# An attention recurrence fused with a Gelu MLP: decays computed in place, another order for the ramp, and two transposes moved to the DMA queue

## The chip, the cores and the metric

The kernel runs on one core of one Trainium2 chip. The metric is the device time of one execution, in microseconds, and a time quoted below is a median of several executions. TensorE is called PE, its weight loads PEld, VectorE DVE, ScalarE ACT, GpSimd POOL, and SyncE (which issues every DMA here) SP. Runs have a fast and a slow state (slower by over 1.5%, or at a lower granted clock). All ratios below are of fast runs; a median may hold a slow run, and then the text says so.

## The reference

A decaying key-value state is updated for every time step, read by `r`, and the result goes through a two-layer MLP. Shapes: 4 batches, 8 heads, 768 steps, head dimension 48; the MLP is 384 to 2048 to 384.

```python
for t in range(S):
    cur = einsum('bhd,bhe->bhde', u * k[t], v[t])
    y[t] = einsum('bhd,bhde->bhe', r[t], state + cur)
    state = w[t][..., None] * state + einsum('bhd,bhe->bhde', k[t], v[t])
x = y.transpose(0, 2, 1, 3).reshape(B * S, H * D)      # 3072 x 384
h = x @ w_in
g = 0.5 * h * (1.0 + tanh(c * (h + 0.044715 * h**3)))  # Gelu
out = g @ w_out
```

## The kernel before

The work is cut into 12 units, each of 256 time steps of one batch. Each of the 128 partitions holds an even and an odd step (`t2` = 0 and 1). A unit has an attention half and an MLP half. The MLP half of unit q (`mm1`, Gelu, `mm2`) is interleaved on PE with the attention half of unit q+1 (steps a2 to a6), and the decays of a later unit are prepared beside both.

The decays become exponentials of cumulative sums of log w. `x` sums up to before the even step, `y` through the even step, `z` through the odd step. `k` is scaled by exp(-y) or exp(-z), `r` by exp(x) or exp(y):

```python
    def a1(q):
        lw = logws[q % 3]
        x, y, z = (ps_a.tile([P, 512], FP, tag="a", name=f"cum{q}_{i}") for i in range(3))
        for dst, s0, s1 in ((x, strict, strict), (y, incl, strict), (z, incl, incl)):
            PE.matmul(dst[:, 0:HD], s0, lw[:, 0, :, 0:D], start=True, stop=False)
            PE.matmul(dst[:, 0:HD], s1, lw[:, 1, :, 0:D], start=False, stop=True)
        for g in range(G):
            for t2 in range(2):
                PE.matmul(z[:, ds(HD + 2 * g, 2)], lw[:, t2, ds(2 * g, 2), :], ones2,
                          start=False, stop=(t2 == 1), skip_group_check=True)
        st["cum", q] = (x, y, z)

    def exps(q):            # cut: the tiles fq, e1 and al are in SBUF
        ...
        ACT.activation(out=e1[:, 0, :], in_=y[:, 0:HD], func=AF.Exp, scale=-1.0)
        ACT.activation(out=e1[:, 1, :], in_=z[:, 0:HD], func=AF.Exp, scale=-1.0)
        ACT.activation(out=fq[:, 0, :], in_=x[:, 0:HD], func=AF.Exp)
        ACT.activation(out=fq[:, 1, :], in_=y[:, 0:HD], func=AF.Exp)
        ACT.activation(out=al, in_=z[:, ds(HD, 2 * G)].rearrange("p (g c) -> p g c", c=2),
                       func=AF.Exp)
            # cut

    def prep(q):            # cut
        ...
        DVE.tensor_tensor(out=kk[:, :, :, 0:D], in0=tdh(kt), in1=dec(e1), op=AL.mult)
        DVE.tensor_tensor(out=rq[:, :, :, 0:D], in0=tdh(rt), in1=dec(fq), op=AL.mult)
        # cut: POOL makes vb (a cast of v), rk = r*k*u, and am, the state's decay
        ...

    def prep_b(q):
        kk, rq, vb, vsc, am = st["pre", q]
        rk, dg = st.pop(("diag", q))
        DVE.tensor_reduce(out=dg, in_=rk, axis=AX.X, op=AL.add)
        POOL.tensor_tensor(
            out=vsc, in0=vb,
            in1=dg.rearrange("p h t -> p t h")[:, :, :, None].broadcast_to([P, 2, H, D]),
            op=AL.mult)
```

`kk` and `rq` are transposed on PE through PSUM, and DVE copies the result back:

```python
    def a2(q, which):
        kk, rq, vb, vsc, am = st["pre", q]
        src = (kk, rq)[which]
        ps = ps_a.tile([P, G, 2, 2, 64], BF, tag="a", name=f"T{q}_{which}")
        for g in range(G):
            for t2 in range(2):
                PE.transpose(ps[:, g, :, t2, :], src[:, t2, ds(2 * g, 2), :], ident)
        dst = pw2.tile([P, G, 2, 2, 64], BF, tag=f"T{which}", name=f"TT{q}_{which}")
        DVE.tensor_copy(out=dst, in_=ps)
        st["T", q, which] = dst

```

The first units are the ramp. There the weights still arrive and are cast to bf16, and the order of the program is different (casts of `w_out` follow the whole of `mm1`; the Ln and the sums of unit 2 come last):

```python
    for q in range(NU):
        if q + 3 < NU:
            for nm in ("k", "r", "v"):
                load(q + 3, nm)
        if q + 4 < NU:
            load(q + 4, "w")
        att = attention(q + 1) if q + 1 < NU else iter(())
        table("gelu")
        ramp = q < 2
        if ramp:
            for i in range(8):
                mm1(q, i)
            if q == 0:
                for i in range(8):
                    cast_w_out(i, DVE if i in (0, 3, 6) else (ACT if i in (1, 4, 7) else POOL))
        for i in range(8):
            if not ramp:
                mm1(q, i)
            if i >= 2:
                mm2(q, 0, (2 * i - 4, 2 * i - 3))
            if i in (1, 3, 4, 5, 6, 7):
                next(att, None)
            if i == 6 and 0 < q and q + 2 < NU:
                a1(q + 2)
        table("exp")
        if q == 0:
            ln(2)
            a1(2)
        if q + 2 < NU:
            exps(q + 2)
        # cut: rest of mm2, stores, prep(q + 2), prep_b(q + 2)
```

## Time and profile before

| | before |
|---|---|
| time, median of 3 runs (lowest to highest) | 236.93 us (235.68 to 237.95) |
| span of the profiled run, mean granted clock | 235.9 us, 0.968 |
| PE busy | 203.4 us, 86% |
| distance from one unit's first mm1 matmul to the next, units 4 to 7 | 16.56 us |
| first mm1 matmul of units 0, 1, 2, 3 | 24.78, 53.74, 74.04, 91.34 us |

The page's slice view cuts the span into 40 equal slices. A digit is the busy share in tenths (9 is 90% or more), and PEclk is the granted clock in tenths. Before:

```profile
PE   0456787598895999999999999999999999999992
...
PEclk9999996779997999999999999999999999999998
```

From slice 13 on (the first is slice 0; this is at 77 us) PE is at 9. In slices 6 and 7 (35 to 47 us) and in slice 12 it falls to between 5 and 7, and there the clock is at 6 or 7 tenths. So there are two regimes: a steady one in which PE's own work sets the time, and a ramp in which PE waits and is also slow. The chain of waits, by engine, says the same: PE is only about half of what ended last.

```profile
PE 54%; ACT 19%; DVE 11%; issue 9%; POOL 3%; DMA 2%; DVEq 0%; ACTq 0%; POOLq 0%
ACT L156 5%; DVE w_out_sb L86 2%; DMA w_89<-in_w_dram 2%; PE o_0_532 L354 1%; DVE rq_127 L203 1%; ACT logw_124 L162 1%; PE o_0_3678 L354 1%; PE o_0_3457 L354 1%; PE o_0_3175 L354 1%; PE o_1_3740 L354 1%; PE o_1_3632 L354 1%; PE o_1_3389 L35
```

The first line is the share of the span by engine, the second by line and tile. The second gives 5% to the loading of the Exp table (L156), 2% to DVE casts of `w_out`, and 1% to a Ln (`logw_124`). The table load comes in every unit; the casts are entries of the ramp alone.

The windows view gives one steady unit of before and the 15 us in which the clock is low. Columns: the window and its length, then busy us with the number of instructions in brackets for PE, PEld, DVE, ACT and POOL, then the granted clock, the DMA share and GB/s.

```profile
35.00:40.00 5.00, 3.24 (x56) 1.51 (x56) 4.21 (x7) 0.55 (x1) 1.12 (x2) 0.67 1.10 248
40.00:45.00 5.00, 3.42 (x40) 2.13 (x41) 2.96 (x3) 1.99 (x3) 4.40 (x3) 0.65 1.12 255
...
124.47:141.03 16.56, 15.89 (x210) 11.42 (x208) 10.18 (x17) 10.51 (x20) 8.22 (x6) 1.00 0.54 121
```

A steady unit holds 15.89 us of PE work in 16.56 us. Between 35 and 50 us the clock is two thirds and PE is busy for only 10.5 of 15 us (the third slice, left out, has 3.82 us and 0.69). The Trainium skill, "TensorE: Matmul & The Clock Gate", Part 1: The HAM clock gate, says that the throttled clock is the default and that activity releases it. This trace agrees. From 26.4 us to the end of PE's work, the granted clock is 0.50 in three stretches, which start at 36.67, 46.90 and 74.21 us and last 6.8, 3.4 and 3.4 us. Each starts within 0.8 us of the end of one of PE's three longest waits of that time (2.1 us to 36.68, 2.7 us to 46.18 and 2.4 us to 74.04). Ahead of 26.4 us the column has no record and reads full speed, but PE is slow there too: the matmuls of the first sums start 0.32 us apart (at 5.71 and 6.03 us), and those of unit 2, of the same shape, 0.16 us apart (at 46.18 and 46.34 us).

The two longest of PE's waits between 25 and 74 us (columns: engine, tile and line, who released it; us in total, times, longest) name what the ramp waits for:

```profile
PE cum_0_658 L170 <- ACT logw_124 L162: 2.7, 1, 2.7
PE mt_0_0_537 L249 <- DVE TT_0_530 L238: 2.1, 1, 2.1
```

The first is unit 2's sums waiting for its Ln. The second is the scores of unit 1 waiting for the copy of its transposed tile. On DVE's timeline (start, us, engine, line, operation) that copy stands behind three casts of `w_out`:

```profile
32.50 1.84 DVE L86 CAST w_out_sb<-wo_179 128x768 bf16<-128x768 f32 x1
34.26 1.17 DVE L86 CAST w_out_sb<-wo_187 128x768 bf16<-128x768 f32 x1
35.36 0.68 DVE L238 COPY TT_1_519<-T_1_510 128x1024 bf16<-128x1024 bf16 x1
35.96 0.67 DVE L238 COPY TT_0_530<-T_0_521 128x1024 bf16<-128x1024 bf16 x1
```

These are the second and third cast (the first, 1.09 us, starts at 31.49), and the two copies. The second copy is the one that PE waits for.

In the steady state the trace has two small holes per unit on PE, here in the unit from 124.47 us (the bracket is idle time and what ended it):

```profile
127.19 0.81 PE L345 MATMUL h_2_1987<-xT_1899,w_in_sb 128*128 128x256 bf16 x6 [0.36 <-ACT g_1948 L347]
...
135.36 0.32 PE L170 MATMUL cum_1_2151<-logw_123,incl 128*128 128x384 bf16 x1 [0.31 <-ACT xs_2148 L321]
```

The first, 0.36 us, is mm1's third group waiting for the Gelu to free a PSUM buffer. The second, 0.31 us, is the second of the three sums waiting for a PSUM buffer that ACT reads. The Gelu is late because ACT is in its other table. ACT's timeline of that block:

```profile
121.50 1.28 ACT L156 ACT_TABLE_LOAD   x1
122.80 0.49 ACT L183 ACTIVATE e_1880<-cum_1_1847 128x384 bf16<-128x384 f32 x1
...
125.25 1.28 ACT L158 ACT_TABLE_LOAD   x1
```

From the first table load (121.50) to the end of the second (126.53) ACT is away from the Gelu for 5.0 us.

### The profile page before, as it was taken

The page shows a single profiled execution, that of the slowest core. Times are in us where ns is not written, and L with a number is a line of the kernel's source. Part 1 is how long each engine was busy: PE and PEld are TensorE (multiplying, and loading weights), DVE is VectorE, ACT ScalarE, POOL GpSimd, SP SyncE. Part 2 cuts the span into 40 slices and gives each one's busy share as a digit, 9 for nine tenths or more (in the row PEclk, how much of TensorE's full clock was granted, in tenths as well). Part 3 has the DMA queues.
Part 4 walks back from the last instruction along what each step waited for, and adds up shares of the span by engine and source line. Part 5 has one row for each costly group of instructions (what it writes and reads, how often), then busy time and mean ns, then how long its engine had stood idle before and what let it go on. Part 6 is the DMA issues. An engine that isn't in the chain of part 4 may idle for free.

```text
span 235.9 us, 5759 instructions
## 1 busy us (share of the span) xinstructions
PE 203.4 (86%) x2448; PEld 143.0 (61%) x2448; DVE 131.3 (56%) x211; ACT 134.0 (57%) x223; POOL 104.5 (44%) x87
## 2 busy tenths in 40 slices
PE   0456787598895999999999999999999999999992
PEld 0334564357564767667767667676777677677761
DVE  7684686561636538547547747656285376374200
ACT  3433780566255449459368377395494684765670
POOL 3473792639008504806708509329158076060000
PEclk9999996779997999999999999999999999999998
DMA  7999999713902911942923914915719120020202
GB/s 173 307 396 297 331 320 255 160 33 72 231 15 54 246 25 36 206 98 53 232 56 75 257 24 111 210 33 124 182 35 212 24 62 10 13 56 0 68 1 67
DMA packets 56969, 30.45 MB, mean 129 GB/s; under 512 B 50928, under 2 KB 56176, under 8 KB 56944
## 3 DMA queue, kind: packets, MB, share of 16 engines
q1 hardware_dynamic: 56944, 30.09, 52.1%
q8 instruction: 19, 0.31, 0.6%
q14 instruction: 6, 0.05, 0.1%
HBM read 25.36 MB, written 4.72 MB: 127 GB/s over the span
## 4 chain that ended last, share of the span: by engine, by line
PE 54%; ACT 19%; DVE 11%; issue 9%; POOL 3%; DMA 2%; DVEq 0%; ACTq 0%; POOLq 0%
ACT L156 5%; DVE w_out_sb L86 2%; DMA w_89<-in_w_dram 2%; PE o_0_532 L354 1%; DVE rq_127 L203 1%; ACT logw_124 L162 1%; PE o_0_3678 L354 1%; PE o_0_3457 L354 1%; PE o_0_3175 L354 1%; PE o_1_3740 L354 1%; PE o_1_3632 L354 1%; PE o_1_3389 L354 1%; POOL rk_418 L210 1%; POOL rk_418 L212 1%; ACT logw_122 L162 1%
## 5 line engine op out<-in xcount | busy, mean ns | idle before, releaser
L345 PEld LDWEIGHTS <-w_in_sb 128*128 128x128 bf16 x576 | 54.0, 99 | 21.1 <-issue 9.9
L156 ACT ACT_TABLE_LOAD x13 | 16.7, 1283 | 0.9 <-PEq L487 0.7
L158 ACT ACT_TABLE_LOAD x12 | 15.4, 1283 | 0.2
L171 PEld LDWEIGHTS <-strict 128*128 128x128 bf16 x24 | 2.5, 104 | 9.9 <-issue 9.5
L215 POOL TENSOR_TENSOR am_997<-blk,al_975 128x384 f32<-128x384 bf16 x2 | 2.4, 1230 | 12.5 <-ACT al_975 L187 12.5
L215 POOL TENSOR_TENSOR am_1304<-blk,al_1273 128x384 f32<-128x384 bf16 x2 | 2.4, 1229 | 11.5 <-ACT al_1273 L187 11.5
L215 POOL TENSOR_TENSOR am_1608<-blk,al_1577 128x384 f32<-128x384 bf16 x2 | 2.4, 1230 | 8.3 <-ACT al_1577 L187 8.3
L215 POOL TENSOR_TENSOR am_1912<-blk,al_1881 128x384 f32<-128x384 bf16 x2 | 2.4, 1230 | 8.3 <-ACT al_1881 L187 8.3
L215 POOL TENSOR_TENSOR am_2216<-blk,al_2185 128x384 f32<-128x384 bf16 x2 | 2.4, 1230 | 8.3 <-ACT al_2185 L187 8.3
L215 POOL TENSOR_TENSOR am_2520<-blk,al_2489 128x384 f32<-128x384 bf16 x2 | 2.4, 1228 | 8.3 <-ACT al_2489 L187 8.3
L215 POOL TENSOR_TENSOR am_2811<-blk,al_2780 128x384 f32<-128x384 bf16 x2 | 2.4, 1228 | 7.9 <-ACT al_2780 L187 7.9
L215 POOL TENSOR_TENSOR am_3100<-blk,al_3069 128x384 f32<-128x384 bf16 x2 | 2.4, 1228 | 7.9 <-ACT al_3069 L187 7.9
L215 POOL TENSOR_TENSOR am_3382<-blk,al_3352 128x384 f32<-128x384 bf16 x2 | 2.4, 1228 | 7.9 <-ACT al_3352 L187 7.9
L354 PE MATMUL o_0_532<-w_out_sb,g_437 128*128 128x384 bf16 x16 | 5.5, 469 | 0.2 <-ACT w_out_sb L84 0.2
L236 PEld LDWEIGHTS <-rq_127 128*128 128x128 bf16 x48 | 3.4, 104 | 3.3 <-DVE rq_127 L203 3.2
L354 PEld LDWEIGHTS <-g_437 128*128 128x128 bf16 x32 | 3.3, 117 | 3.2 <-issue 2.5
L170 PE MATMUL cum_0_201<-logw_122,strict 128*128 128x384 bf16 x1 | 0.5, 479 | 5.4 <-ACT logw_122 L162 5.4
L362 DVE COPY ob_3736<-o_0_3678 128x384 f32<-128x384 f32 x1 | 0.6, 558 | 7.7 <-PE o_0_3678 L354 7.7
L215 POOL TENSOR_TENSOR am_699<-blk,al_677 128x384 f32<-128x384 bf16 x2 | 2.3, 1187 | 4.3 <-ACT al_677 L187 4.3
L354 PEld LDWEIGHTS <-g_3653 128*128 128x128 bf16 x32 | 3.0, 98 | 1.7 <-ACT g_3653 L347 0.4
L238 DVE COPY TT_1_818<-T_1_809 128x1024 bf16<-128x1024 bf16 x1 | 0.7, 692 | 6.0 <-PE T_1_809 L236 6.0
L354 PE MATMUL o_0_3678<-w_out_sb,g_3653 128*128 128x384 bf16 x16 | 3.8, 327 | 0.0
(942 smaller groups left out, 694.2 us busy)
## 6 DMA issues: line engine op xcount, KB each, us to landing
wi_155<-in_moe_w_in_dram SPq DMA_DIRECT2D x1, 512.0 KB, 5.0
wi_157<-in_moe_w_in_dram SPq DMA_DIRECT2D x1, 512.0 KB, 6.0
wi_159<-in_moe_w_in_dram SPq DMA_DIRECT2D x1, 512.0 KB, 6.7
wi_161<-in_moe_w_in_dram SPq DMA_DIRECT2D x1, 512.0 KB, 7.5
wi_163<-in_moe_w_in_dram SPq DMA_DIRECT2D x1, 512.0 KB, 8.7
wi_165<-in_moe_w_in_dram SPq DMA_DIRECT2D x1, 512.0 KB, 9.6
w_89<-in_w_dram SPq DMA_DIRECT2D x1, 384.0 KB, 3.7
k_91<-in_k_dram SPq DMA_DIRECT2D x1, 384.0 KB, 4.7
```

The lines of the kernel that those rows point to most:

```text
L86: eng.tensor_copy(out=out, in_=in_)
L156: ACT.preload_act_table_set(EXP_SET)
L158: ACT.preload_act_table(AF.Gelu_apprx_tanh)
L162: ACT.activation(out=lw[:, :, :, 0:D].rearrange("p t h d -> p h t d"), in_=ld.pop(("w", q)).rearrange("p h (t d) -> p h t d", t=2), func=A ...
L171: PE.matmul(dst[:, 0:HD], s1, lw[:, 1, :, 0:D], start=False, stop=True)
L203: DVE.tensor_tensor(out=rq[:, :, :, 0:D], in0=tdh(rt), in1=dec(fq), op=AL.mult)
L210: POOL.tensor_tensor(out=rk, in0=kt.rearrange("p h (t d) -> p h t d", t=2), in1=rt.rearrange("p h (t d) -> p h t d", t=2), op=AL.mult)
L212: POOL.tensor_tensor(out=rk, in0=rk, in1=u_bc[:, :, None, :].broadcast_to([P, H, 2, D]), op=AL.mult)
L215: POOL.tensor_tensor(out=am[:, c2], in0=blk.rearrange("p g j d -> p g (j d)"), in1=al[:, :, c2][:, :, None].broadcast_to([P, G, 2 * D]), o ...
L236: PE.transpose(ps[:, g, :, t2, :], src[:, t2, ds(2 * g, 2), :], ident)
L345: PE.matmul(h[:, f, :], w_in_sb[:, cb, ts(ft, P)], xT[:, cb, :], start=(f + cb == 0), stop=(cb == NCB - 1), skip_group_check=True)
L354: PE.matmul(st["o", q, c2], g[:, ft, ts(c2, P)], w_out_sb[:, ft, :], start=(ft == 0), stop=(ft == NFT - 1))
```

## The change

It has four parts.

1. Two sums and two large Exps instead of three and four. Because y = z - log w(odd) and y = x + log w(even), exp(-y) is exp(-z) times w(odd), and exp(y) is exp(x) times w(even). So `y` is not needed; instead `kw` = k(even) * w(odd) and `rw` = r(odd) * w(even) are computed, on POOL from unit 5 on. With it, mm2 of the unit is moved back by two mm1 groups, so that more PE work follows the table switch.
2. The Exps of all units but unit 5 write in place in PSUM, and DVE's multiplies read them there: four of 384 elements per partition instead of two of 768.
3. The ramp has an order of its own: the decays come earlier, the casts of `w_out` lie between the phases of the attention, loads are issued earlier, and mm1 is interleaved. In the loop behind the ramp, decays run three units ahead instead of two.
4. From unit 6 on (`PE_T`) `kk` and `rq` are transposed by the DMA, issued from SP, instead of by PE and a DVE copy.

The core of the diff; layouts, indices, loads, the start and much of the ramp loop are cut.

```diff
-        x, y, z = (ps_a.tile([P, 512], FP, tag="a", name=f"cum{q}_{i}") for i in range(3))
-        for dst, s0, s1 in ((x, strict, strict), (y, incl, strict), (z, incl, incl)):
-            PE.matmul(dst[:, 0:HD], s0, lw[:, 0, :, 0:D], start=True, stop=False)
-            PE.matmul(dst[:, 0:HD], s1, lw[:, 1, :, 0:D], start=False, stop=True)
+        x, z = ((pool or ps_a).tile([P, 512], FP, tag=tag, name=f"cum{q}_{i}") for i in range(2))
+        for dst, tri in ((x, strict), (z, incl)):
+            for t2 in range(2):
+                PE.matmul(dst[:, 0:HD], tri, lw[:, t2, :, 0:D], start=(t2 == 0),
+                          stop=(t2 == 1))
-        st["cum", q] = (x, y, z)
-
-    def exps(q):
-        x, y, z = st.pop(("cum", q))
-        fq = pw2.tile([P, 2, HD], BF, tag="fq", name=f"fq{q}")
-        e1 = pw2.tile([P, 2, HD], BF, tag="e1", name=f"e1{q}")
-        al = pw2.tile([P, G, 2], FP, tag="al", name=f"al{q}")
-        ACT.activation(out=e1[:, 0, :], in_=y[:, 0:HD], func=AF.Exp, scale=-1.0)
-        ACT.activation(out=e1[:, 1, :], in_=z[:, 0:HD], func=AF.Exp, scale=-1.0)
-        ACT.activation(out=fq[:, 0, :], in_=x[:, 0:HD], func=AF.Exp)
-        ACT.activation(out=fq[:, 1, :], in_=y[:, 0:HD], func=AF.Exp)
-        ACT.activation(out=al, in_=z[:, ds(HD, 2 * G)].rearrange("p (g c) -> p g c", c=2),
-                       func=AF.Exp)
-        st["dec", q] = (fq, e1, al)
         # cut
+    def prep_w(q, eng=POOL):
+        wt, kt, rt = (ld[nm, q] for nm in ("w", "k", "r"))
+        # cut
+        eng.tensor_tensor(out=kw, in0=kt[:, :, 0:D], in1=wt[:, :, D:2 * D], op=AL.mult)
+        eng.tensor_tensor(out=rw, in0=rt[:, :, D:2 * D], in1=wt[:, :, 0:D], op=AL.mult)
         # cut
+    def exps(q, sbuf=False):
+        x, z = (t[:, 0:HD] for t in st["cum", q])
+        zf = st.pop(("cum", q))[1]
+        fq, e1 = x, z
+        if sbuf:
+            fq, e1 = (pw2.tile([P, HD], BF, tag=t, name=f"{t}{q}", bufs=1) for t in ("fq", "e1"))
+        al = pw2.tile([P, G, 2], FP, tag="al", name=f"al{q}", bufs=3)
+        ACT.activation(out=e1, in_=z, func=AF.Exp, scale=-1.0)
+        ACT.activation(out=fq, in_=x, func=AF.Exp)
         # cut
-        DVE.tensor_tensor(out=kk[:, :, :, 0:D], in0=tdh(kt), in1=dec(e1), op=AL.mult)
-        DVE.tensor_tensor(out=rq[:, :, :, 0:D], in0=tdh(rt), in1=dec(fq), op=AL.mult)
+        for dst, t2, x, dec in ((kk, 0, kw, e1), (kk, 1, kt[:, :, D:2 * D], e1),
+                                (rq, 0, rt[:, :, 0:D], fq), (rq, 1, rw, fq)):
+            DVE.tensor_tensor(out=dst[:, :, t2, :, 0:D], in0=gjd(x),
+                              in1=dec.rearrange("p (g j d) -> p g j d", g=G, j=2),
+                              op=AL.mult)
         # cut: a2
+        if q < PE_T[which]:
+            # cut: the transposes on PE and the copy, as before
+            return
+        for c2 in range(2):
+            SP.dma_start(out=dst[:, c2].rearrange("p g t x -> p (g t) x"),
+                         in_=src[ds(64 * c2, 64)].rearrange("p g t j d -> p (g t j d)"),
+                         transpose=True)
         # cut
+    for q in range(3):
+        att = attention(q + 1)
+        table("gelu")
+        for i in range(6):
+            mm1(q, i)
+        if q == 0:
+            wo(0, DVE)
+        next(att)
+        mm1(q, 6)
+        mm1(q, 7)
+        table("exp")
+        prep_b(q + 1)
+        if q > 0:
+            prep_a(2 * q + 1)
+        if q == 2:
+            prep_w(5)
+        if q == 0:
+            wo(1, DVE)
+        if q == 0:
+            ln(2)
+        next(att)
+        if q == 0:
+            wo(2, DVE)
+            wo(3, POOL)
+        mm2(q, 0, (0, 1))
+        next(att)
+        mm2(q, 0, range(2, 6))
+        if q == 0:
+            wo(4, DVE)
+            wo(5, POOL)
+        next(att)
+        mm2(q, 0, range(6, 10))
+        next(att)
+        mm2(q, 0, range(10, 12))
         # cut: rest of the ramp loop
+    for q in range(3, NU):
         att = attention(q + 1) if q + 1 < NU else iter(())
         table("gelu")
         # cut
         for i in range(8):
+            mm1(q, i)
-            if i >= 2:
-                mm2(q, 0, (2 * i - 4, 2 * i - 3))
+            if i >= 4:
+                mm2(q, 0, (2 * i - 8, 2 * i - 7))
         # cut
```

## The prediction

> **What bounds the kernel now.** From about 91 us on, TensorE does. The slice row shows PE at 9 tenths from there; the windows give it 9.3 to 10.0 us busy in each 10, ACT 4.3 to 8.3, DVE 4.5 to 7.0. Units start 16.56 us apart (h_0 in PE's timeline). At start-to-start times a unit needs: mm1 8 x 0.655 = 5.24, mm2 32 x 0.163 = 5.2, cumulative sums 1.2, transposes of kk and rq 0.9, scores 0.7, y and p2 1.3, state products and output transposes 0.7: about 15.2. The other 1.3 us are holes: 0.4 waiting for the Gelu, behind five Exp, a Ln and two table loads (5.0 us of ACT); 0.5 waiting for a PSUM buffer in the third sum; small gaps.
>
> Before that the ramp bounds. mm1 of units 0 to 3 starts at 24.8, 53.7, 74.0 and 91.3 us. In the chain of waits unit 1 waits for rk on POOL (2.5 + 2.4 us), a reduce, three w_out casts ahead of the transposed copies on DVE, then unit 2's Ln, sums, Exps and multiplies in a row; the granted clock is 0.65-0.69 from 35 to 50 us.
>
> **What changes.**
> 1. Two sums instead of three: -0.32 us of PE per unit. Two Exp fewer: -0.75 us of ACT, whose block shrinks to about 4.2 us; 5.5 us of PE work now follow the switch, so the Gelu hole closes.
> 2. Exps in PSUM: DVE does four 384-wide multiplies (estimate 0.56 us each, as the state's PSUM reads) for two of 0.96: off the path. POOL gets 1.9 us more, with room. The sums hold PSUM longer; they should be free just as the next scores need them.
> 3. Ramp: unit 1's multiplies before the first mm1, w_out casts spread between phases, rk late. Estimate: mm1 at 22, 44, 62, 80 us; 11 us gained.
> 4. DMA transposes for six units: -0.9 us of PE, -1.3 us of DVE each. A unit moves four pieces of 128 KB. The Trainium skill, "DMA: Bandwidth & Descriptors", Latency and other measured facts, gives 261 GB/s for one such kernel: an estimate of 2 us, plus landing like this trace's 2.2 us for stores. Issued a unit (14 us) ahead, they should hide. This trace has none to check it.
>
> **Sum.** Units 3 and 4 at 15.4 us, 5 to 8 at 14.4, 9 and 10 at 13.3, the last with its stores 14.7: 129.7 us after 80, plus 1 from span to time: **211 us**, range 203 to 222. Faster by over 2%: 0.94; within 2%: 0.04; slower: 0.02. PE's savings from unit 3 on are on the critical path; ACT's and DVE's count only where they close holes.
>
> **Right would show as** units 14.0-14.7 us apart from unit 5, 15-15.6 before; PE at 9 tenths; no wait for transposed tiles; unit 3's mm1 near 80 us; no 0.67 clock at 35-50 us; each transpose issue well under 3 us. **Wrong as** scores waiting for a DMA, or for DVE to release a sum's PSUM; mm1 waiting for the Gelu in its first four groups, now without mm2 between (0.655 against 0.5 to 0.6 us).
>
> **What would make it wrong.** DMA transposes costing SP 4 us or more apiece: stores and loads behind them in the queue fall back, and units grow to 16-20 us. A ramp bound by loads: eight more are issued early. PE staying slow through the ramp. A new PSUM wait of 0.5 us per unit costs 4 us.

## The result, and the profile after

| | before | after |
|---|---|---|
| time, median of 4 runs each (lowest to highest) | 236.31 us (235.39 to 237.95) | 208.19 us (206.82 to 208.43) |
| ratio of the fast runs, 95% interval | | 0.8792 (0.8726 to 0.8858) |
| span of the profiled run, clock | 235.9 us, 0.968 | 206.3 us, 0.996 |
| PE busy | 203.4 us, 86% | 184.5 us, 89% |
| unit to unit, steady | 16.56 us | 14.15 us, later 13.30 us |
| first mm1 matmul of units 0, 1, 2, 3 | 24.78, 53.74, 74.04, 91.34 us | 22.82, 41.90, 58.01, 75.89 us |

Ratios here and below are the mean time of one kernel's fast runs over that of the other's fast runs of the same rounds, so they are not quite the ratio of the medians quoted.

Of the 29.6 us of span, 91.34 - 75.89 = 15.45 us were gained before unit 3's first matmul, and the other 14.15 us after it. After, slices and chain:

```profile
PE   0566697998999897999999999999999999999991
...
PEclk9999999999999999999999999999999999999998
...
PE 75%; DVE 15%; POOL 3%; DMA 2%; ACT 2%; issue 1%; DVEq 0%; ACTq 0%; POOLq 0%
```

PE stands at 8 or 9 from slice 7 on (36 us), but for a 7 in slice 15 (77 to 83 us), of which more below, and the granted clock is at 9 in all slices but the last. In the chain PE rose from 54% to 75% and ACT fell from 19% to 2%. The same 15 us as above, and one steady unit:

```profile
35.00:40.00 5.00, 4.64 (x71) 3.25 (x70) 3.97 (x8) 2.44 (x6) 2.11 (x3) 1.00 1.12 253
40.00:45.00 5.00, 4.94 (x38) 3.55 (x37) 4.23 (x8) 3.38 (x6) 4.92 (x4) 1.00 1.07 254
...
121.94:136.10 14.16, 14.16 (x193) 10.33 (x191) 9.13 (x18) 9.80 (x17) 9.38 (x9) 1.00 0.88 178
```

The clock is full (here the pace agrees: mm1 groups start 0.65 us apart at 41.90 and 42.55 us), and the steady unit has no idle time on PE that this view shows: 14.16 us of work in 14.16 us. ACT's block between two Gelus is 4.26 us (104.05 to 108.31) instead of 5.03:

```profile
104.05 1.28 ACT L157 ACT_TABLE_LOAD   x1
105.34 0.47 ACT L220 ACTIVATE cum_1_1900<-cum_1_1900 128x384 f32<-128x384 f32 x1
...
107.03 1.28 ACT L159 ACT_TABLE_LOAD   x1
```

The new DMA transposes, on SP's timeline for the first of these units, and one of them in the view of that source line (nanoseconds min/median/max of one issue, then the landing in us):

```profile
92.33 2.61 SPq L259 DMA_TRANSPOSE TT_0_1654<-kk_125  x2
```

```profile
L259 SPq DMA_TRANSPOSE TT_0_1961<-kk_126 x2: 1220/1245/1270, 107.4 to 108.7; - x2
...
DMA to landing us min/median/max: 2.7/2.8/4.4
```

A unit issues four pieces of 128 KB, each about 1.24 us, so SP's queue is taken for about 5.1 us of a unit's 14.15. A piece lands 2.8 us after its issue by the median (4.4 at most). It is needed a unit later, and the list of PE's waits has no wait for one.

### The profile page after: what moved, and what is told of

Same layout as the page of the kernel before. It is cut to its first block, busy times and chain, and to the rows that moved or that the text cites. A ratio compares the mean times of both kernels' runs of the same rounds, so it can differ in the third digit from the quotient of the medians.

```text
span 206.3 us, 5543 instructions
## 1 busy us (share of the span) xinstructions
PE 184.5 (89%) x2328; PEld 132.9 (64%) x2328; DVE 129.1 (63%) x223; ACT 123.9 (60%) x197; POOL 114.2 (55%) x114
## 4 chain that ended last, share of the span: by engine, by line
PE 75%; DVE 15%; POOL 3%; DMA 2%; ACT 2%; issue 1%; DVEq 0%; ACTq 0%; POOLq 0%
DMA w_89<-in_w_dram 2%; PE o_1_3620 L378 1%; PE o_0_1489 L378 1%; PE o_0_2921 L378 1%; PE o_0_2373 L378 1%; PE o_0_2088 L378 1%; PE o_0_3574 L378 1%; PE o_0_2656 L378 1%; PE o_0_3396 L378 1%; PE o_1_3512 L378 1%; PE o_1_3292 L378 1%; PE o_1_3072 L378 1%; PE o_1_2808 L378 1%; PE o_1_2537 L378 1%; PE o_1_2252 L378 1%; PE o_1_1967 L378 1%
## 5 line engine op out<-in xcount | busy, mean ns | idle before, releaser
L157 ACT ACT_TABLE_LOAD x13 | 16.7, 1283 | 0.9 <-PEq L585 0.7
L159 ACT ACT_TABLE_LOAD x12 | 15.4, 1283 | 0.2
L172 PEld LDWEIGHTS <-strict 128*128 128x128 bf16 x24 | 1.8, 100 | 6.6 <-issue 4.9
L378 PEld LDWEIGHTS <-g_440 128*128 128x128 bf16 x32 | 2.8, 97 | 3.0 <-issue 1.4
L378 PE MATMUL o_0_558<-w_out_sb,g_440 128*128 128x384 bf16 x16 | 3.6, 327 | 1.1 <-DVE w_out_sb L86 1.1
L378 PEld LDWEIGHTS <-g_3533 128*128 128x128 bf16 x32 | 3.1, 98 | 1.6
L378 PEld LDWEIGHTS <-g_2829 128*128 128x128 bf16 x32 | 3.1, 98 | 1.5
L378 PEld LDWEIGHTS <-g_1689 128*128 128x128 bf16 x32 | 3.1, 98 | 1.5
L378 PEld LDWEIGHTS <-g_1375 128*128 128x128 bf16 x32 | 3.1, 98 | 1.5
L378 PEld LDWEIGHTS <-g_2281 128*128 128x128 bf16 x32 | 3.1, 98 | 1.5
L378 PEld LDWEIGHTS <-g_2564 128*128 128x128 bf16 x32 | 3.1, 98 | 1.5
L378 PEld LDWEIGHTS <-g_3313 128*128 128x128 bf16 x32 | 3.1, 98 | 1.5
L378 PEld LDWEIGHTS <-g_1996 128*128 128x128 bf16 x32 | 3.1, 98 | 1.5
L378 PEld LDWEIGHTS <-g_3093 128*128 128x128 bf16 x32 | 3.1, 98 | 1.5
L207 POOL TENSOR_TENSOR vsc_530<-vb_434,dg_529 128x768 bf16<-128x768 bf16 x1 | 1.7, 1662 | 4.3 <-DVE dg_529 L206 4.3
L378 PEld LDWEIGHTS <-g_745 128*128 128x128 bf16 x32 | 2.8, 98 | 1.7
L172 PEld LDWEIGHTS <-incl 128*128 128x128 bf16 x24 | 2.5, 106 | 2.0 <-issue 0.7
L378 PEld LDWEIGHTS <-g_1046 128*128 128x128 bf16 x32 | 2.7, 97 | 1.6
L242 POOL TENSOR_TENSOR am_708<-blk,al_680 128x384 f32<-128x384 bf16 x2 | 1.9, 987 | 2.9 <-ACT al_680 L222 2.9
```

The source lines that it names most:

```text
L157: ACT.preload_act_table_set(EXP_SET)
L159: ACT.preload_act_table(AF.Gelu_apprx_tanh)
L172: PE.matmul(dst[:, 0:HD], tri, lw[:, t2, :, 0:D], start=(t2 == 0), stop=(t2 == 1))
L207: POOL.tensor_tensor(out=vsc, in0=vb, in1=dg.rearrange("p h t -> p t h")[:, :, :, None].broadcast_to([P, 2, H, D]), op=AL.mult)
L242: POOL.tensor_tensor(out=am[:, c2], in0=blk.rearrange("p g j d -> p g (j d)"), in1=al[:, :, c2][:, :, None].broadcast_to([P, G, 2 * D]), o ...
L378: PE.matmul(st["o", q, c2], g[:, ft, ts(c2, P)], w_out_sb[:, ft, :], start=(ft == 0), stop=(ft == NFT - 1))
```

## The experiments

Twelve kernels ran; all gave correct results. All were timed in at least four executions. Parts of the change were undone in the after-kernel, or done alone in the before-kernel. After itself was not timed again beside them, so a difference from after rests on the two ratios to before and on the gaps in the traces more than on the two medians. Distances between units are read from DVE's copies to `xT` (one per unit), because they can be found in every trace. They differ in the ramp from distances between first mm1 matmuls. Each list starts with the gap from unit 0 to unit 1. In after they are 16.95, 16.12, 16.12, 18.67, 14.01, 14.80, 14.16, 14.15, 14.15, 13.30 and 13.30 us. The first three below and the one with the Exps in SBUF ran together, beside 7 runs of before (median 237.78 us).

### All transposes back on PE

```diff
@@
-    PE_T = (6, 6)
+    PE_T = (12, 12)
```

> The changed kernel with the DMA transposes undone: units 6 to 11 are transposed on TensorE and copied by DVE, as units 0 to 5 are. Theory (TensorE is the limit, so what it no longer does comes off the time): each of the six units grows by the 0.9 us of transposes, and by the 0.5 to 0.8 us hole that the changed kernel shows in units 3 and 4 where the scores wait for the DVE copies; 5.4 to 9 us in all, so 213.5 to 217 us, and units 5 to 10 start 15.0 to 15.5 us apart instead of 14.15. Rival (the order of the steady loop and the shorter ACT block made the gain, the transposes would hide): under 2 us, so 208 to 210 us.

Measured: 215.46 us, ratio to before 0.9074 (0.9045 to 0.9102). The gaps up to unit 5 are unchanged within 0.2 us, then 15.40, 15.39, 15.40, 15.39, 14.54, 14.54 us: 0.60 us more for the first of the six and 1.24 for each other. A unit in the windows view:

```profile
119.12:134.51 15.39, 15.11 (x208) 11.21 (x207) 10.41 (x18) 9.78 (x17) 9.34 (x9) 1.00 0.59 130
```

PE's work in the unit is 15.11 us, 0.95 more than after's 14.16, and 0.28 us of the unit are idle. The theory held. So the DMA transposes are worth the matmuls that they take away and a small hole besides, in which PE waits for DVE's copy.

### A third sum with its two Exps put back

Results of the added sum are thrown away; only its cost matters.

```diff
@@
+        if q >= 6:
+            y = ps_a.tile([P, 512], FP, tag="a", name=f"cumy{q}")
+            st["cumy", q] = y
+            for t2 in range(2):
+                PE.matmul(y[:, 0:HD], (incl, strict)[t2], lw[:, t2, :, 0:D], start=(t2 == 0),
+                          stop=(t2 == 1))
@@
+        if q >= 6:
+            y = st.pop(("cumy", q))
+            yx = pw2.tile([P, 2, HD], BF, tag="yx", name=f"yx{q}")
+            for i, sc in enumerate((-1.0, 1.0)):
+                ACT.activation(out=yx[:, i, :], in_=y[:, 0:HD], func=AF.Exp, scale=sc)
```

> The changed kernel with the removed work put back for units 6 to 11 alone: a third sum (two matmuls of 384 columns) in its own PSUM buffer and two more Exps of it into a scratch tile that nothing reads. The output stays right. Theory: TensorE's 0.33 us comes back for each of the six units, 2 us, and the longer ACT block (5.0 us) still hides behind the 5.5 us of matmuls that now follow the table switch: 210 to 211 us. Rival (the shorter ACT block is worth as much as the matmuls): 0.7 us or more a unit, over 212 us, with waits of mm1 for the Gelu in the trace.

Measured: 210.80 us, ratio 0.8876 (0.8847 to 0.8905). Steady gaps 14.67 to 14.68 us, 0.52 us more than after; the matmuls of the sum itself are 0.32 us. Of the other 0.20 us, 0.15 are idle time of PE (14.52 us busy in 14.67) and 0.05 are busy time. The theory's 210 to 211 us held, and PE's list has no wait for a Gelu.

### The order of mm2 put back

```diff
@@
-            if i >= 4:
-                mm2(q, 0, (2 * i - 8, 2 * i - 7))
+            if i >= 2:
+                mm2(q, 0, (2 * i - 4, 2 * i - 3))
@@
-        mm2(q, 0, range(8, 12))
```

> The changed kernel with mm2 of units 3 to 11 interleaved with mm1 from the third group on, as before, so that 4 instead of 8 matmuls of it follow the table switch. Theory: with the ACT block down to 4.2 us the 4.9 us of TensorE work left behind the switch still cover it: within 1 us of the changed kernel. Rival (moving mm2 behind the switch is what closed the Gelu hole): 0.4 us or more a unit, 3 us slower in all, 211 us or more.

Measured: 208.35 us, ratio 0.8770 (0.8742 to 0.8798), steady gaps 14.22 us: 0.06 us more than after. By itself the order is worth nothing that the times show.

### Both together

```diff
@@
+        if q >= 6:
+            y = ps_a.tile([P, 512], FP, tag="a", name=f"cumy{q}")
+            st["cumy", q] = y
+            for t2 in range(2):
+                PE.matmul(y[:, 0:HD], (incl, strict)[t2], lw[:, t2, :, 0:D], start=(t2 == 0),
+                          stop=(t2 == 1))
@@
+        if q >= 6:
+            y = st.pop(("cumy", q))
+            yx = pw2.tile([P, 2, HD], BF, tag="yx", name=f"yx{q}")
+            for i, sc in enumerate((-1.0, 1.0)):
+                ACT.activation(out=yx[:, i, :], in_=y[:, 0:HD], func=AF.Exp, scale=sc)
@@
-            if i >= 4:
-                mm2(q, 0, (2 * i - 8, 2 * i - 7))
+            if i >= 2:
+                mm2(q, 0, (2 * i - 4, 2 * i - 3))
@@
-        mm2(q, 0, range(8, 12))
```

> The changed kernel with the third sum and two more Exps put back for units 6 to 11 (alone: +0.52 us a unit) and mm2 interleaved early in units 3 to 11 (alone: +0.06 us a unit), together. Theory (either a short ACT block or mm2 behind the switch closes the Gelu hole, so only undoing both opens it): units 5 to 8 at 15.1 to 15.3 us instead of 14.15, with mm1 waiting for the Gelu about 0.4 us a unit; total 212 to 214 us. Rival (the two simply add): 14.7 us a unit, 210.5 to 211.5 us.

Measured (another round; before 236.32 us): 214.25 us, ratio 0.9058 (0.8998 to 0.9118). Steady gaps 15.32 to 15.33 us: 1.18 us more than after, while the parts alone add up to 0.58. PE's timeline has the hole again:

```profile
143.19 0.81 PE L380 MATMUL h<-xT,w_in_sb 128*128 128x256 bf16 x6 [0.79 <-ACT g L382]
```

An mm1 group waits 0.79 us for the Gelu. The theory of two cures holds, with time and hole a little above its ranges. Either of the two, the shorter ACT block or the mm2 work left behind the table switch, nearly closes that hole. Without both it opens. The steady unit now adds up: 14.15 + 1.18 (sums, Exps and order) + 1.24 (transposes) = 16.57, and before has 16.56.

### The Exps back in SBUF

```diff
@@
-        if sbuf:
-            fq, e1 = (pw2.tile([P, HD], BF, tag=t, name=f"{t}{q}", bufs=1) for t in ("fq", "e1"))
+        if True:
+            fq, e1 = (pw2.tile([P, HD], BF, tag=t, name=f"{t}{q}", bufs=2) for t in ("fq", "e1"))
```

> The changed kernel with the two exponentials of every unit written to bfloat16 tiles in SBUF (two buffers each) instead of in place in PSUM. Theory (in-place exponentials are off the critical path; they save SBUF, not time): within 1 us of the changed kernel's 208.2, ACT's Exp 0.48 against 0.47 us each, DVE's multiplies the same 0.54 us. Rival 1 (PSUM in place is what made ACT and DVE faster): 2 to 4 us slower. Rival 2 (keeping the sums in PSUM until the multiplies costs a wait): 1 to 3 us faster.

My theory was that the place of the Exps' output is off the critical path. Measured: 216.21 us, ratio 0.9111 (0.9069 to 0.9154): 8 us slower than after (7.5 by the ratios, 8.0 by the spans). The theory fell, and the loss is larger than either rival had it. The gaps are 16.88, 17.22, 17.17, 20.00, 17.96, 14.80, 14.15 us and so on: the loss lies between unit 1 and unit 5 (and 0.6 us at the start), and steady units are unchanged.

The source view of DVE's multiplies in this run (two of its four lines; min/median/max in ns):

```profile
L237 DVE TENSOR_TENSOR kk<-kw,e x12: 553/882/2158, 8.1 to 170.5; 128x384 bf16<-128x384 f32 x12
L237 DVE TENSOR_TENSOR kk<-k,e x12: 544/552/2162, 8.6 to 170.9; 128x384 bf16<-128x384 f32 x12
```

The same instruction takes 0.54 us at best and 2.16 us at worst. In after every multiply with its decay in PSUM took 0.54 to 0.56 us. The sum over a stretch of the ramp, after first (windows view of DVE for that line alone: busy us with the number of instructions, clock, DMA share, GB/s), then this run:

```profile
40.00:57.00 17.00, 1.93 (x4) 1.00 1.04 247
```

```profile
40.00:57.00 17.00, 5.81 (x4) 1.00 1.07 251
```

1.93 us became 5.81 us for the same four multiplies. What stretches them can be seen inside the after-kernel itself, because it puts the Exps of one unit, unit 5, in SBUF. DVE's first two multiplies of that unit, then POOL's instruction at that time:

```profile
86.68 1.21 DVE L237 TENSOR_TENSOR kk_127<-kw_1143,e_1321 128x384 bf16<-128x384 f32 x1
87.81 0.54 DVE L237 TENSOR_TENSOR kk_127<-k_736,e_1321 128x384 bf16<-128x384 f32 x1
```

```profile
85.86 1.62 POOL L242 TENSOR_TENSOR am_1558<-blk,al_1322 128x384 f32<-128x384 bf16 x2
```

The first multiply starts while POOL works on `am` (until 87.48) and takes 1.21 us. The second has the same shape, also has both inputs in SBUF, and takes 0.54 us, with POOL idle from 87.48 to 90.30. Now a multiply with its decay in PSUM that lies beside a POOL multiply; DVE, then POOL:

```profile
107.72 0.55 DVE L237 TENSOR_TENSOR rq_129<-rw_1721,cum_0_1899 128x384 bf16<-128x384 f32 x1
```

```profile
107.94 1.00 POOL L187 TENSOR_TENSOR kw_2005<-k_1680,w_1372 128x384 f32<-128x384 f32 x1
```

It takes 0.55 us. The same holds for all multiplies of both traces. In after, all 44 with the decay in PSUM lie beside a POOL instruction, and none is stretched. In the run with all Exps in SBUF, the 10 of 48 that meet no POOL instruction take 0.54 to 0.55 us, and the 24 that take 1.17 us or more all meet one. So the stretching was seen only with both: two inputs in SBUF, and POOL at work. Both together are not always enough: the other 14 also lie beside a POOL instruction by the trace, whose POOL spans are rough, and take less than 0.6 us. Two rivals fall with these numbers: the type of the decays (bf16 in SBUF, f32 in PSUM) makes no difference where POOL is idle, and no Exp of this run waited for one of its two SBUF buffers (ACT's list of waits). The Trainium skill, "SBUF — State Buffer", Who interferes with whom, states this: a DVE instruction with two SBUF inputs contends with a GpSimd instruction that reads SBUF, and one with at most one SBUF input, outside the 2-port modes, does not. The trace agrees. It fits before as well: there the `rq` multiply took 1.58, 2.56 and 1.58 us in the first three units, each beside POOL, and 0.95 us in all later ones (some of these lie beside POOL's `am` too). In the steady state of this run the multiplies are stretched too (3.23 us for four, from 124 to 138 us), but DVE has room there, and it costs nothing. In the ramp the multiplies stand ahead of PE's transposes, and there each unit pays. The largest loss, 3.95 us in the gap from unit 4 to unit 5, is not the multiplies' length alone: PE waits 2.6 us for the copy behind them, and from 102.87 to 106.29 us the granted clock is 0.50 with PE busy throughout, which is up to 1.7 us more (an estimate: half of 3.42 us).

### The ramp: order on DVE alone, Ln and sums alone, and both, in the before-kernel

Two candidates for the ramp's gain: DVE's order (the wait for the copy behind the casts, 2.1 us), which the prediction's reading of the chain names ahead of the Ln, and the early Ln and sums of unit 2 (the wait of 2.7 us). Three kernels, run together with the last of all below (before: 236.30 us, 11 runs, one of them slow).

DVE order alone, first try:

```diff
@@
-    prep_b(1)
@@
-                for i in range(8):
-                    cast_w_out(i, DVE if i in (0, 3, 6) else (ACT if i in (1, 4, 7) else POOL))
+                wo = lambda *ii: [cast_w_out(i, DVE if i in (0, 3, 6) else
+                                             (ACT if i in (1, 4, 7) else POOL)) for i in ii]
+                wo(0, 1, 4, 7)
+                next(att)
+                prep_b(1)
+                wo(2, 5)
@@
-            if i in (1, 3, 4, 5, 6, 7):
+            if q == 0 and i == 3:
+                wo(3)
+            if q == 0 and i == 4:
+                wo(6)
+            if i in ((3, 4, 5, 6, 7) if q == 0 else (1, 3, 4, 5, 6, 7)):
```

> The kernel before with one thing reordered in its first unit: unit 1's reduce, and all but one of DVE's three w_out casts, come after the copies of unit 1's transposed tiles on DVE instead of ahead of them. Theory (DVE's order kept TensorE waiting): the transposed copies end near 31.5 instead of 36.6 us and unit 1's mm1 starts 3 to 5 us earlier than 53.7; total 232 to 234 us. Rival (the first unit is bound by the loads or by the serial Ln, sums and Exps behind it): under 1.5 us.

Measured: 237.54 us, ratio 1.0058 (0.9989 to 1.0126). No gain, but the try was flawed. I had moved a POOL cast of `w_out` behind a POOL multiply that waits for the reduce, and PE then waited for it:

```profile
38.21 0.48 PE L354 MATMUL o<-w_out_sb,g 128*128 128x384 bf16 x2 [3.34 <-POOL w_out_sb L86]
```

Early Ln and sums alone:

```diff
@@
+        if q == 0:
+            table("exp")
+            ln(2)
@@
-            if i == 6 and 0 < q and q + 2 < NU:
+            if i == 6 and q + 2 < NU:
@@
-        table("exp")
-        if q == 0:
-            ln(2)
-            a1(2)
+        if q > 0:
+            table("exp")
```

> The kernel before with unit 2's table switch and Ln directly behind the Gelus of unit 0, and its sums after unit 1's first state product, as in all later units, instead of both behind unit 1's last state product. DVE's order is as before. Theory (decays computed just in time held up mm2 of unit 0): unit 1's mm1 starts 2.5 to 4 us earlier; total 232.5 to 234.5 us. Rival: under 1.5 us.

Measured: 231.56 us, ratio 0.9792 (0.9732 to 0.9853), which is unclear against a threshold of 2% but not against no effect. The gap from unit 0 to 1 is 25.73 us, where before has 30.11, and the wait of the sums for the Ln is no longer in PE's list. The gap fell by 4.4 us, more than the 2.7 us of the wait and than the 2.5 to 4 us of the theory. The clock may be the rest: of before's three stretches at 0.50 (13.65 us) this run has only one, from 37.9 to 44.7 us. This was not tested by itself.

Both:

```diff
@@
-    prep_b(1)
@@
-                for i in range(8):
-                    cast_w_out(i, DVE if i in (0, 3, 6) else (ACT if i in (1, 4, 7) else POOL))
+                wo = lambda *ii: [cast_w_out(i, DVE if i in (0, 3, 6) else
+                                             (ACT if i in (1, 4, 7) else POOL)) for i in ii]
+                wo(0, 1, 4, 7)
+                next(att)
+                prep_b(1)
+                wo(2, 5)
+        if q == 0:
+            table("exp")
+            ln(2)
@@
-            if i in (1, 3, 4, 5, 6, 7):
+            if q == 0 and i == 3:
+                wo(3)
+            if q == 0 and i == 4:
+                wo(6)
+            if i in ((3, 4, 5, 6, 7) if q == 0 else (1, 3, 4, 5, 6, 7)):
@@
-            if i == 6 and 0 < q and q + 2 < NU:
+            if i == 6 and q + 2 < NU:
@@
-        table("exp")
-        if q == 0:
-            ln(2)
-            a1(2)
+        if q > 0:
+            table("exp")
```

> Both edits of the first unit in the kernel before. Theory (the two waits follow each other, so they add): unit 1's mm1 starts 6 to 9 us earlier, near 46 us, and the granted clock of 0.65-0.69 from 35 to 50 us is gone or shorter; total 227 to 230 us. Rival 1 (one hides behind the other): no more than the better of the two alone. Rival 2 (the changed kernel's ramp gained from its multiplies ahead of use in units 1 and 2 rather than from unit 0): total above 232 us.

Measured: 233.28 us, ratio 0.9873 (0.9816 to 0.9930), with the first try's flaw in it.

The DVE order was mended by leaving all of the POOL and ACT casts where they were (another round; before 236.32 us, 7 runs):

```diff
@@
-    prep_b(1)
@@
-                for i in range(8):
-                    cast_w_out(i, DVE if i in (0, 3, 6) else (ACT if i in (1, 4, 7) else POOL))
+                wo = lambda *ii: [cast_w_out(i, DVE if i in (0, 3, 6) else
+                                             (ACT if i in (1, 4, 7) else POOL)) for i in ii]
+                wo(0, 1, 2, 4, 5, 7)
+                next(att)
+                prep_b(1)
@@
-            if i in (1, 3, 4, 5, 6, 7):
+            if i in ((3, 4, 5, 6, 7) if q == 0 else (1, 3, 4, 5, 6, 7)):
@@
+            if q == 0 and i == 3:
+                wo(3)
+            if q == 0 and i == 5:
+                wo(6)
```

> The kernel before with DVE's order in unit 0 changed as in the first try, but without its flaw: there a w_out cast on POOL had come to stand behind the reduce, and TensorE waited 3.3 us for it. Now POOL casts before, and DVE's second and third cast come behind the masks and the state. Theory: copies of unit 1 end near 34.5 instead of 36.6 us, unit 1's mm1 2 to 3 us earlier than 53.7, total 233 to 235 us. Rival (this order is covered by a later wait): under 1 us.

Measured: 235.45 us, ratio 0.9946 (0.9877 to 1.0015), so the interval includes no effect. PE's waits between 25 and 76 us show why:

```profile
PE cum L170 <- ACT logw L162: 2.7, 1, 2.7
...
PE o L354 <- DVE w_out_sb L86: 1.6, 1, 1.6
...
PE mt L249 <- DVE TT L238: 0.3, 1, 0.3
```

The wait for the copies fell from 2.1 to 0.3 us, as intended, but a wait of 1.6 us for a DVE cast took its place, and a wait for a Gelu grew from 1.2 to 1.9 us. The wait for the Ln stayed at 2.7 us. The rival won: the casts were on the chain, but behind them stood waits that were nearly as long.

Both, mended:

```diff
@@
-    prep_b(1)
@@
-                for i in range(8):
-                    cast_w_out(i, DVE if i in (0, 3, 6) else (ACT if i in (1, 4, 7) else POOL))
+                wo = lambda *ii: [cast_w_out(i, DVE if i in (0, 3, 6) else
+                                             (ACT if i in (1, 4, 7) else POOL)) for i in ii]
+                wo(0, 1, 2, 4, 5, 7)
+                next(att)
+                prep_b(1)
+        if q == 0:
+            table("exp")
+            ln(2)
@@
-            if i in (1, 3, 4, 5, 6, 7):
+            if i in ((3, 4, 5, 6, 7) if q == 0 else (1, 3, 4, 5, 6, 7)):
@@
-            if i == 6 and 0 < q and q + 2 < NU:
+            if q == 0 and i == 3:
+                wo(3)
+            if q == 0 and i == 5:
+                wo(6)
+            if i == 6 and q + 2 < NU:
@@
-        table("exp")
-        if q == 0:
-            ln(2)
-            a1(2)
+        if q > 0:
+            table("exp")
```

> That mended order and the early Ln and sums of unit 2 together, in the kernel before. Early Ln alone gave 5 us. Theory (two waits, one behind the other): unit 1's mm1 near 46.5 us, 7 us earlier than before, total 227.5 to 230 us. Rival: no better than the early Ln alone, 231 to 232 us.

Measured: 234.38 us, ratio 0.9912 (0.9831 to 0.9992): less gain than with the early Ln alone (0.9792, other rounds), and less than either the theory or its rival had. In its trace PE waits 2.49 us for a cast of `w_out` on DVE that took 2.15 us. PE, then DVE:

```profile
46.01 0.80 PE L354 MATMUL o<-w_out_sb,g 128*128 128x384 bf16 x2 [2.49 <-DVE w_out_sb L86]
```

```profile
43.80 2.15 DVE L86 CAST w_out_sb<-wo 128x768 bf16<-128x768 f32 x1
```

The cast took 2.15 us here, where two of DVE's casts in after run in 0.55 us (31.82 and 38.17 us) and two more in 0.64 and 0.74; here it lies beside POOL's multiplies of `rk` (41.65 to 45.53 us). That it is the overlap which stretches the cast was read from this one place, not tested.

The other way round: both ramp items put back into the after-kernel.

```diff
@@
+    prep_b(1)
@@
+            wo(1, DVE)
+            wo(2, DVE)
@@
-        table("exp")
-        prep_b(q + 1)
+        if q > 0:
+            table("exp")
+            prep_b(q + 1)
@@
-        if q == 0:
-            wo(1, DVE)
-        if q == 0:
-            ln(2)
@@
-            wo(2, DVE)
@@
+        if q == 0:
+            table("exp")
+            ln(2)
```

> The changed kernel with the order of its first unit put back: unit 1's reduce and three w_out casts on DVE ahead of unit 1's transposed copies, and the table switch, Ln and sums of unit 2 behind unit 1's last state product. Everything else as changed. Theory (these two orders are most of the 9.9 us by which unit 0 became shorter): unit 0 grows from 16.95 to 23-26 us between copies of xT, total 214 to 217 us. Rival (multiplies ahead and in PSUM made the gain in unit 0): under 3 us, below 211.5 us.

Measured: 212.86 us (5 runs, one of them, the profiled one, slow), ratio of the fast runs 0.8975 (0.8907 to 0.9044), where after has 0.8792: some 4 to 5 us. The result lies between the ranges of the theory and of the rival. The profile is slow, so only the kind of its waits is used: the wait of the sums for the Ln is back in PE's list, 2.7 us as in before.

### A next version: unit 4's products earlier

Unit 3 of after, from its first mm1 matmul to unit 4's, is 16.50 us long where the prediction had 15.4. PE's and DVE's timelines show why:

```profile
77.53 0.82 PE L369 MATMUL h_1_1415<-xT_1294,w_in_sb 128*128 128x256 bf16 x6
79.64 0.24 PE L272 MATMUL mt_0_0_1423<-TT_1_1395,TT_0_1384 48*64 48x128 bf16 x2 [1.30 <-DVE TT_1_1395 L255]
...
79.99 0.83 PE L369 MATMUL h_2_1444<-xT_1294,w_in_sb 128*128 128x256 bf16 x6
```

```profile
73.37 1.84 DVE L188 TENSOR_TENSOR rw_1332<-r_211,w_201 128x384 f32<-128x384 f32 x1
...
76.99 0.94 DVE L206 TENSOR_REDUCE dg_1342<-rk_1139 128x16 f32<-128x768 f32 x1
...
78.91 0.68 DVE L255 COPY TT_1_1395<-T_1_1396 128x1024 bf16<-128x1024 bf16 x1
```

PE waits 1.30 us for the second copy of unit 4's transposed tiles. Before it on DVE stand `rw` with two SBUF inputs, 1.84 us beside POOL's work, and a reduce. This kernel gives `kw` and `rw` of unit 4 to POOL half a unit earlier (with a third buffer for each) and moves unit 5's reduce into a gap of DVE:

```diff
@@
-        kw = pw2.tile([P, H, D], FP, tag="kw", name=f"kw{q}")
-        rw = pw2.tile([P, H, D], FP, tag="rw", name=f"rw{q}")
+        kw = pw2.tile([P, H, D], FP, tag="kw", name=f"kw{q}", bufs=3)
+        rw = pw2.tile([P, H, D], FP, tag="rw", name=f"rw{q}", bufs=3)
@@
+        if q == 1:
+            prep_w(4)
@@
-        prep_w(q + 2, DVE)
+        if q < 2:
+            prep_w(q + 2, DVE)
@@
-        if q == 2:
-            prep_b(5)
-        else:
+        if q < 2:
@@
+            if q == 3 and i == 2:
+                prep_b(5)
```

> The changed kernel with two moves at unit 2's end, where the trace shows DVE late for unit 4's transposed copies and TensorE waiting 1.8 us: unit 4's products with the decay go to POOL half a unit earlier (on DVE they took 2.9 us beside POOL's), and unit 5's reduce moves into a DVE gap of unit 3. Theory: unit 3 shrinks from 16.5 to 15.0-15.5 us, total 206.5 to 207.3 us. Rival (something else behind DVE holds unit 3): no change, 208.2.

Measured (the round of 11 before-runs): 206.45 us (205.99 to 206.87, 6 runs), ratio 0.8728 (0.8691 to 0.8765). Between first mm1 matmuls unit 3 is now 15.39 us (75.27 to 90.66), in the theory's range. By the copies to `xT` the gap of 18.67 us became 16.85, the next grew from 14.01 to 14.73, and the span is 204.5 us against 206.3. By medians it is 0.8% faster than after. The two were not timed in the same rounds and the intervals of their ratios overlap a little, so the gain rests on the gaps in the trace more than on the times. It is the fastest of all kernels run.

## Why the prediction was right or wrong

**The time.** 211.0 us was predicted, and 208.19 measured; the direction, the range and most of the mechanism held. The difference has these terms. Unit 3's mm1 was put at 80 us and came at 75.89: 4.1 us. The sum after it was put at 129.7 and was 130.4: -0.7 us. From span to time 1 us was added, where the profiled run has 208.06 - 206.3 = 1.8: -0.8 us. The rest is the profiled run against the median and rounding.

**Step 1, sums and Exps: right.** ACT's block was put at about 4.2 us and is 4.26. The 0.32 us of PE are in the trace. The test of the parts adds one thing: the closing of the Gelu hole has two causes, each nearly sufficient alone. The feared wait of mm1's first groups did not come.

**Step 2, Exps in PSUM "off the path": wrong in what it left out.** The multiplies are 0.54 to 0.56 us, as predicted. But the step treated the place of the output as neutral, and it is worth 8 us of this version's time, most of it because it takes DVE out of the way of POOL (the slow clock in unit 4 may be up to 1.7 us of it). The prediction had the evidence before it: the `rq` multiply in before took 0.95 us in the steady state and up to 2.56 in the first units. Compared with the before-kernel this is part of the ramp's gain: in the version with Exps in SBUF, unit 3's copy to `xT` came 2.7 us later than in after (74.12 against 71.41).

**Step 3, the ramp: right in direction, mis-sized.** 11 us were predicted and 15.45 gained. The mis-sized terms are unit 0 (44 - 22 = 22 us predicted, 19.1 measured) and unit 1 (18 and 16.1). Unit 2 held (18 and 17.9), the start was 0.8 us later than put, and 44, 62 and 80 thus became 41.9, 58.0 and 75.9. What the runs isolate of the 15.45 us: the early Ln and sums alone gave before about 5 us; undoing these and the order of the casts costs after 4 to 5 us; the PSUM operand accounts for 2.7 us up to unit 3. The casts ahead of the copies, which the prediction read from the chain of waits, gave 0.9 us alone, with no effect inside the interval. The rest (DVE's `kk`, `rq` and reduce no longer ahead of unit 2's copy to `xT`, for which PE waited 2.4 us in before; mm1 interleaved; loads issued earlier; the earlier first unit) was read from traces and not isolated. How it divides stays open. The clock runs through all of these terms, and the step names it only as a sign. In before PE was busy for 13.48 of the 13.65 us in which the granted clock was 0.50, all of them ahead of unit 3's first matmul. If all that work ran at half pace, the slow clock cost up to 6.7 us (an estimate: half of 13.48). After has no such stretch between its first clock record at 27.3 us and its last 2 us. These 6.7 us are not to be added to the terms above: before's slow stretches follow its waits, so what shortens the waits may also bring the faster clock, and no run here separates the two.

**The clock: right.** No window from 35 to 50 us is below 1.00 after, and the pace of the matmuls confirms it.

**Step 4, DMA transposes: right in the result, the queue's time mis-sized.** From the 261 GB/s of the skill's page the estimate was 2 us of transfer per unit. SP issued the four pieces in about 5 us. It was far from the 4 us apiece that would have hurt, and it hid behind the unit. The gain was put at 0.9 us of PE; it is 0.95 and a 0.28 us hole.

**Steady units: right.** 14.4 us were predicted for units 5 to 8 and 14.15 measured; 13.3 for 9 and 10, and 13.3 measured. Unit 3 was 1.1 us longer than put (16.5 against 15.4), for the reason seen in the last experiment, and the last unit 0.6 us (15.3 against 14.7).

## What to carry to other kernels

When DVE multiplies stand ahead of the bottleneck while POOL works, look at the spread of one instruction's durations: if the longest are twice the shortest, ask whether both of its inputs are in SBUF, and whether one can be left in PSUM. A wait that the chain of waits names is worth its length only if nothing of nearly that length stands behind it, so try it alone before counting it. It may also be worth more than its length, where the clock falls with it. Check the clock by the pace of equal matmuls. Work that PE does and another engine can do a unit ahead (here transposes on the DMA queue) is worth its full time once PE has no other holes, and a short hole may have two independent cures, of which one is enough.

## What the Trainium skill lacked or had wrong

- "DMA: Bandwidth & Descriptors", Latency and other measured facts, gives 261 GB/s for a DMA transpose of one kernel, and no issue time; a vendor table further up that page has sequencer cycles for other sizes and "previous generations", not given as measured on trn2. Here each SBUF-to-SBUF transpose of 128 KB kept SP for about 1.24 us (12 pairs, medians 1.23 to 1.80 us), so one queue issued at most 128 KB / 1.24 us = 106 GB/s; the landing was 2.7 to 4.4 us. That is less than half of the page's rate, though it is the issue and not the transfer that was measured.
- "VectorE: DVE Perf Modes", Rules for kernel authors, says of elementwise work on a matmul's output to accept the slow mode or to copy from PSUM to SBUF first where there are many operations. It lacks the other side, which follows only from the rule of the SBUF page cited above: with POOL at work a PSUM operand kept these multiplies at 0.54 us, where SBUF operands took up to 2.16 us, and the place was worth 8 us of the whole.
- "ScalarE: Activation LUTs", What ACT_TABLE_LOAD costs, gives 1283 ns for the load, which the trace confirms (1283 ns, the mean of all 25 loads), and a further drain of about 1380 ns at every switch, which these traces do not show: in after the last Gelu ends at 104.03 us, the load starts at 104.05, and the first Exp at 105.34, so a switch cost 1.3 us.
- "TensorE: Matmul & The Clock Gate", Part 1: The HAM clock gate, warns that clock events in a trace are not to be fully trusted. It does not tell that a profile can lack them at its start: the first clock record lies at 26.4 us in before and at 27.3 us in after, and ahead of it this profile's column reads full speed. After's window from 24 to 27 us reads 1.00, but the six matmuls of an mm1 group took 1.48 us at 24.05 us and 0.82 us at 27.60 us:

```profile
24.05 1.48 PE L369 MATMUL h_1_449<-xT_414,w_in_sb 128*128 128x256 bf16 x6
27.60 0.82 PE L369 MATMUL h_4_473<-xT_414,w_in_sb 128*128 128x256 bf16 x6
```
